# New duration estimates for DMA issues and for per-partition operands in a kernel that orders its own instructions

## The chip, the cores and the metric

The kernel runs on one core of a Trainium2 chip. The metric is the time of one execution on the device in microseconds (us), as the median of several runs. A profile is one execution seen by the hardware profiler. TensorE appears in it as PE (matmuls) and PEld (weight loads), VectorE as DVE, ScalarE as ACT, GpSimd as POOL, and SyncE, which issues all DMAs of this kernel, as SP.

## The reference

The reference is a bucketed attention followed by a mixture of four attention experts, for 4 batches, 8 heads, 768 positions, head size 64:

```
# attention: q, k, v are (4, 8, 768, 64); proj is (64, 6)
mask = bucket(q @ proj > 0)[..., :, None] == bucket(k @ proj > 0)[..., None, :]
scores = where(mask, q @ k.T / 8, -1e9)
x = softmax(scores) @ v            # heads side by side: (4, 768, 512)
# mixture: 4 experts, causal attention, the best 2 of 4 count
logits = x @ w_gate
for e in range(4):
    a = softmax(where(causal, -1e9, (x @ wq[e]) @ (x @ wk[e]).T / 8))
    ye = a @ (x @ wv[e]) @ wo[e]
    out += (weight of e among the two best gates, else 0) * ye
```

## The kernel before

**Units.** The work is cut into units: 32 L units (one head of one batch of the first attention) and 16 M units (one expert of one batch). For each unit TensorE computes the scores twice: once to find the row maxima (tile mx, reduced by VectorE into pm), once transposed (tile st) for the exponentials (p and ph by ScalarE, their difference pl by GpSimd), and then the product with V (tile o), which VectorE divides (xp, yn). Numbers are kept as a half-precision part and a remainder, so a product takes three matmuls.

**Preparation of a pair of heads.** For a pair, natq, natk and natv are loaded from DRAM (`load`; the load of natv may not come before the preparation of another pair has made its tile M, which `nc.gate` ensures). `pair_scales` reduces natq, natk and natv to their largest magnitudes (mqk) on VectorE and passes these through TensorE (tile misc) to a scale cs. `prep_pair` transposes and scales q and k; VectorE's scalar_tensor_tensor reads the scale as a per-partition operand. `signs` makes M, with two such operands, and sends four pieces of it by DMA into the qk tiles. `halves` sends eight copies from qk to qk. `shift_steps` sends the maxima (row) and flags (fr) by DMA. An M unit (`proj_steps`) has five transfers of its own, the constant rows01 and four copies. Results leave through ot, p32 or Tq.

**The order of the instructions.** Nothing of this is run as it is written down. Every call is recorded as an operation with its predecessors; then `schedule` lists the operations for the five engines. It keeps a time at which each engine comes free, takes the operation that can start earliest on it (ties by program order with some offsets), and adds the operation's estimated cost, which is `_cost`. The order in which operations were taken is the order in which each engine runs them. So an estimate never changes an instruction's real duration; it changes what is listed before what. Some copies have two engines to choose from (`copy`, `choose`), and that choice also goes by the estimated times.

A DMA's estimate has two parts. The issue takes SP's time, which is the part that is edited. The transfer then lands after

```
            free[e] = end = st + cost
            if o.dma is not None:
                dma = end = max(dma, st + 1275.0) + o.dma
                end += 900.0
```

counted from st, the start of its issue. For a load of natv (384 KB in pieces of 256 bytes) `o.dma` is 2,185 ns by the formula in `add`, and a reader on another engine adds 60 and 75 ns, which makes 4.50 us from issue to use. On the chip each engine runs its list strictly in order: if an operation's input is late, everything listed behind it on that engine waits as well.

In the profile every instruction carries the line at which the listed operations are issued (L423), so that groups are told apart by tiles: `qk<-M` reads M and writes qk.

Of the kernel before, what the change touches and what calls it, by code (L numbers as in the profile page):

```python
# [156 lines left out]
def _n(v):  # L157
    return prod(v.shape[1:])


def _cost(rec, eng, name, out, ins, args, kw):
    if name == "dma_start":
        return 650.0
    n = max([_n(out)] + [_n(x) for x in ins[:1]]) if eng != "tensor" else _n(out)
    psum = any(x.tile.space for x in ins if isinstance(x, View))
    if eng == "tensor":
        w = ins[0].dtype
        if name == "transpose":
            return 112.0
        if w == FT:  # L170
            return max(216.0, n * 1.68) / (4 if kw.get("tile_position") else 1)
        if w == FR:
            return max(107.0, n / 2.4 + 3)
        return max(28.0, n / 2.4 + 3) / (4 if kw.get("tile_position") else 1)
    ptr = sum(1 for x in list(args[2:]) + list(kw.values())
              if isinstance(x, View) and x.dtype == FT and prod(x.shape) == x.shape[0])
    if name == "reg_load":
        return 250.0
    if eng == "scalar":
        return (51.0 if psum else 93.0) + 0.833 * n + 93 * ptr  # L180
    if eng == "vector":
        if name == "memset" or (not psum and len([x for x in ins if _n(x) > 1 or n == 1]) < 2
                                and name != "tensor_reduce" and out.dtype != HF):
            return 66.0 + n / 1.92 + 60 * ptr
        return 64.0 + n / 0.96 + 20 * ptr
    if eng == "gpsimd":
        if name == "tensor_tensor":
            return (135.0 if n == 128 else 80.0 + (-0.36 * n if out.tile.name in ("xp", "yn") else 0.0)) + (2.0 if out.dtype == HF else 2.2) * n
        if name == "memset":
            return 36.0 + 0.83 * n if out.dtype in (FT, FR) and n > 200 else 40.0 + 0.1 * n  # L190
        return 190.0 + 2.0 * n
    raise ValueError(eng)
# [12 lines left out]
class Recorder:  # L205
# [21 lines left out]
    def add(self, alts):  # L227
# [9 lines left out]
        o.prio = o.i  # L237
        o.tag = self.tag
        o.alts = [(e, m, a, k, _cost(self, e, m, o.outs[0] if o.outs else None, o.ins, a, k)) for e, m, a, k in alts]
        o.dma = None  # L240
        o.bias = POOL_BIAS
# [1240 lines left out]
```

## Time and profile before

| | |
|---|---|
| time, median of 3 runs | 654.75 us (652.87 to 656.1) |
| the profiled execution's own time | 658.51 us |
| its span, first to last instruction | 656.5 us |
| mean granted TensorE clock | 0.994 of full speed |
| PE busy | 625.3 us, 95% of the span |
| DVE, ACT, POOL busy | 78%, 77%, 70% |
| DMA queue's packets | 32.1% of the 16 engines' time |

Sums of waits and durations below come from the profiled execution, and are then set against the median. A wait in the profile is idle time of an engine just before an instruction, with the event that ended it.

### The profile page before, as it was taken

How to read it: one execution, taken by the hardware profiler on the slowest of the kernel's cores; microseconds unless marked ns; L12 is line 12 of the kernel's file. 1: busy time of each engine (PE TensorE's matmuls, PEld its weight loads, DVE VectorE, ACT ScalarE, POOL GpSimd, SP SyncE). 2: the span in 40 equal slices, each digit the busy share in tenths (PEclk: the TensorE clock that was granted, in tenths of full speed). 3: DMA queues.
4: the chain of work that ended last, by engine and by line, in shares of the span. 5: the costliest groups of instructions: out<-in, count | busy, mean ns of one | idle time of the engine just before them, and what ended most of it. 6: DMA issues, size and time to landing. Idle time of an engine off the chain costs nothing.

```text
span 656.5 us, 21599 instructions
## 1 busy us (share of the span) xinstructions
PE 625.3 (95%) x8297; PEld 459.5 (70%) x8297; DVE 512.1 (78%) x1303; ACT 503.6 (77%) x1106; POOL 462.0 (70%) x509
## 2 busy tenths in 40 slices
PE   8989999898999999999999989899999999999996
PEld 7877767665767676776667767677776766767663
DVE  4997999998779797968879777886977968437653
ACT  3299988998969798867868869685985977952774
POOL 4099988997959686956957769774893867970550
PEclk9999999999999999999999989989999999999999
DMA  4682554443411505032342333305044121001212
GB/s 104 146 176 66 108 118 102 99 100 88 107 41 29 120 19 132 19 84 65 67 116 75 69 78 67 87 15 132 12 89 126 44 70 26 4 19 34 79 66 97
DMA packets 110883, 50.88 MB, mean 77 GB/s; under 512 B 89388, under 2 KB 106940, under 8 KB 110780
## 3 DMA queue, kind: packets, MB, share of 16 engines
q1 hardware_dynamic: 110780, 49.50, 32.1%
q8 instruction: 65, 1.06, 0.7%
q14 instruction: 38, 0.31, 0.2%
HBM read 20.98 MB, written 6.29 MB: 42 GB/s over the span
## 4 chain that ended last, share of the span: by engine, by line
PE 63%; DVE 15%; DMA 10%; ACT 4%; issue 3%; SPq 3%; POOL 1%; DVEq 0%; POOLq 0%; ACTq 0%
PE misc L423 21%; PE st L423 16%; PE o L423 16%; PE mx L423 10%; DVE pm L423 6%; DMA natv<-in_v_dram 5%; SPq L423 3%; DMA qk<-M 2%; ACT p L423 2%; DVE qk L423 2%; DVE mqk L423 2%; ACT ph L423 1%; DVE misc L423 1%; DMA natk<-in_k_dram 1%; POOL pl L423 1%
## 5 line engine op out<-in xcount | busy, mean ns | idle before, releaser
L423 POOL TENSOR_TENSOR pl<-p,ph 128x512 f16<-128x512 f32 x379 | 418.9, 1128 | 169.5 <-ACT ph L423 77.1
L423 ACT ACTIVATE p<-st 128x512 f32<-128x512 f32 (+2 forms) x384 | 227.0, 593 | 53.3 <-PE st L423 45.2
L423 DVE TENSOR_REDUCE pm<-mx 128x2 f32<-128x512 f32 (+2 forms) x380 | 226.9, 615 | 16.9 <-PE mx L423 15.6
L423 PE MATMUL st<-qk 78*128 78x512 f16 (+2 forms) x976 | 228.0, 324 | 1.9 <-ACT ph L423 0.8
L423 ACT ACTIVATE ph<-st 128x512 f16<-128x512 f32 (+2 forms) x384 | 227.0, 596 | 0.5 <-PE o L423 0.4
L423 PEld LDWEIGHTS <-ph 128*128 128x128 f16 x2976 | 157.8, 98 | 27.7 <-issue 3.8
L423 PEld LDWEIGHTS <-qk 78*128 78x128 f16 (+4 forms) x1392 | 124.0, 98 | 62.2 <-issue 10.4
L423 PE MATMUL mx<-qk 76*128 76x512 f16 (+2 forms) x488 | 136.1, 325 | 5.9 <-DVE pm L423 3.1
L423 PEld LDWEIGHTS <-pl 128*128 128x128 f16 x1488 | 136.2, 97 | 5.0 <-issue 1.5
L423 PE MATMUL o<-vh,ph 128*128 128x65 f16 (+1 forms) x1152 | 125.7, 194 | 0.6 <-DVE xp L423 0.4
L423 PE MATMUL o<-vh,pl 128*128 128x65 f16 (+1 forms) x1152 | 125.5, 193 | 0.6 <-POOL pl L423 0.6
L423 PE MATMUL o<-vl,ph 128*128 128x64 f16 x1152 | 125.3, 192 | 0.1
L423 PE MATMUL misc<-xt,wqk_h 128*128 128x384 f16 x256 | 53.7, 326 | 1.3 <-DVE ytl L423 1.3
L423 PEld LDWEIGHTS <-ident 128*128 128x128 bf16 x460 | 36.2, 102 | 13.1 <-issue 2.8
L423 DVE SCALAR_TENSOR_TENSOR qk<-misc,qk 128x384 f16<-128x384 f32 (+1 forms) x34 | 18.7, 552 | 27.0 <-ACT qk L423 26.9
L423 PE MATMUL o<-mvh,ph 128*128 128x65 f16 x336 | 37.7, 195 | 0.6 <-DVE yn L423 0.6
L423 PEld LDWEIGHTS <-xt 128*128 128x128 f16 x324 | 30.3, 97 | 11.3 <-issue 1.0
L423 PE MATMUL o<-mvh,pl 128*128 128x65 f16 x336 | 37.6, 195 | 0.0
L423 PE MATMUL o<-mvl,ph 128*128 128x64 f16 x336 | 37.6, 193 | 0.0
L423 ACT ACTIVATE qk<-misc 128x384 f16<-128x384 f32 (+1 forms) x33 | 16.2, 490 | 27.2 <-PE misc L423 24.1
L423 PEld LDWEIGHTS <-wqk_h 128*128 128x128 f16 x256 | 24.2, 97 | 15.4 <-issue 1.0
L423 DVE SCALAR_TENSOR_TENSOR qk<-misc,cs,qk 128x384 f16<-128x384 f32 x56 | 33.2, 604 | 1.3 <-ACT qk L423 1.2
(188 smaller groups left out, 930.1 us busy)
## 6 DMA issues: line engine op xcount, KB each, us to landing
qk<-qk SPq DMA_DIRECT2D x128, 96.0 KB
natv<-in_v_dram SPq DMA_DIRECT2D x16, 384.0 KB
natq<-in_q_dram SPq DMA_DIRECT2D x15, 384.0 KB
natk<-in_k_dram SPq DMA_DIRECT2D x15, 384.0 KB
qk<-qk SPq DMA_DIRECT2D x112, 48.0 KB
out_dram<-ot SPq DMA_DIRECT2D x20, 256.0 KB
xt<-xt SPq DMA_DIRECT2D x8, 96.0 KB
xt<-xt SPq DMA_DIRECT2D x4, 192.0 KB
```

The lines of the kernel that those rows point to most:

```text
L423: getattr(getattr(self.nc, e), m)(*[real(x) for x in args], **{k: real(x) for k, x in kw.items()})
```

## The change

No operation is added or removed. Two estimates in `_cost` are edited: the SP time of a DMA's issue, one constant before, now depends on the tile that is read; and each per-partition fp32 operand of a VectorE instruction that falls under the last line of that branch adds 60 ns where it added 20. Loads from DRAM have no tile that is read, and fall under 570.

```
     if name == "dma_start":
-        return 650.0
+        of = ins[0].tile.name if ins else ""
+        return 930.0 if of in ("M", "Mw") else 700.0 if of[:3] in ("row", "fr") else 340.0 if of in ("ot", "p32") else 570.0
...
-        return 64.0 + n / 0.96 + 20 * ptr
+        return 64.0 + n / 0.96 + 60 * ptr
```

## Rows read from the trace of the kernel before

**Rows 1.** The page: busy time of each engine, and share of the span.
```profile
PE 625.3 (95%) x8297; PEld 459.5 (70%) x8297; DVE 512.1 (78%) x1303; ACT 503.6 (77%) x1106; POOL 462.0 (70%) x509
```

**Rows 2.** Waits of PE: total us, times, longest us.
```profile
PE misc L423 <- DVE mqk L423: 4.5, 3, 2.8
PE misc L423 <- DVE row L423: 3.4, 3, 1.5
PE mx L423 <- DVE pm L423: 3.1, 10, 0.7
PE mx L423 <- DMA qk<-M: 1.6, 3, 1.1
```

**Rows 3.** Waits of DVE: total us, times, longest us.
```profile
DVE mqk L423 <- DMA natv<-in_v_dram: 15.9, 10, 3.2
DVE mqk L423 <- DMA natq<-in_q_dram: 6.1, 6, 2.2
```

**Rows 4.** Chain of work that ended last, near one natv: start us, us, what.
```profile
382.56 0.60 SPq L423
...
383.20 4.09 DMA natv<-in_v_dram
...
387.32 0.97 DVE mqk L423
...
388.33 0.23 PE misc L423
```

**Rows 5.** Windows around ten natv waits: length, PE, PEld, DVE, ACT, POOL busy, PEclk, DMA.
```profile
384.00:390.00 6.00, 3.17 (x49) 2.18 (x46) 2.81 (x7) 2.40 (x7) 3.89 (x4) 0.97 0.42 94
...
sum 62.00, PE 49.41 PEld 34.06 DVE 42.08 ACT 38.06 POOL 39.65; mean PE 4.94 PEld 3.41 DVE 4.21 ACT 3.81 POOL 3.97
```

**Rows 6.** SP's issues before that natv: start us, us, tiles, count.
```profile
368.69 5.98 SPq L423 DMA_DIRECT2D qk<-M  x4
374.71 2.45 SPq L423 DMA_DIRECT2D qk<-qk  x4
377.27 0.71 SPq L423 DMA_DIRECT2D qk<-row  x1
378.10 5.06 SPq L423 DMA_DIRECT2D qk<-qk  x7
383.20 0.59 SPq L423 DMA_DIRECT2D natv<-in_v_dram  x1
```

**Rows 7.** SP's issues before the natv at 116 us.
```profile
111.08 3.66 SPq L423 DMA_DIRECT2D qk<-M  x4
114.78 0.66 SPq L423 DMA_DIRECT2D qk<-row  x1
115.49 0.64 SPq L423 DMA_DIRECT2D fq<-fr  x1
116.17 0.40 SPq L423 DMA_DIRECT2D natv<-in_v_dram  x1
```

**Rows 8.** SP's issues before the natv at 177 us.
```profile
169.73 3.66 SPq L423 DMA_DIRECT2D qk<-M  x4
173.45 3.50 SPq L423 DMA_DIRECT2D qk<-qk  x4
176.99 0.59 SPq L423 DMA_DIRECT2D natv<-in_v_dram  x1
```

**Rows 9.** SP's issues before the natv at 297 us.
```profile
285.59 4.42 SPq L423 DMA_DIRECT2D qk<-M  x4
290.06 0.66 SPq L423 DMA_DIRECT2D qk<-row  x1
290.76 5.03 SPq L423 DMA_DIRECT2D qk<-qk  x8
295.84 0.79 SPq L423 DMA_DIRECT2D qk<-rows  x1
296.68 0.42 SPq L423 DMA_DIRECT2D natv<-in_v_dram  x1
```

**Rows 10.** DVE groups by shape: out<-in, count | busy us, mean ns | idle before.
```profile
L423 DVE SCALAR_TENSOR_TENSOR qk<-misc,cs,qk 128x384 f16<-128x384 f32 x56 | 33.2, 604 | 1.3 <-ACT qk L423 1.2
...
L423 DVE SCALAR_TENSOR_TENSOR qk<-misc,qk 128x384 f16<-128x384 f32 x32 | 17.7, 552 | 26.9 <-ACT qk L423 26.9
```

**Rows 11.** Issues of stores from ot: ns min/median/max, first and last start.
```profile
L423 SPq DMA_DIRECT2D out_dram<-ot x20: 332/338/537, 334.8 to 651.9; - x20
```

**Rows 12.** Windows behind two natv waits: PE busy, ..., PEclk (granted clock).
```profile
388.00:394.00 6.00, 5.61 (x62) 3.89 (x63) 5.24 (x16) 3.12 (x8) 2.55 (x3) 0.72 0.02 3
426.00:432.00 6.00, 5.34 (x58) 3.84 (x58) 5.04 (x16) 4.07 (x10) 2.67 (x3) 0.72 0.02 5
```

## The prediction

> **What bounds the kernel now.** I read the page's busy times first. TensorE is busy 625.3 of 656.5 us [rows 1]: 31.2 us are all that a better order could win, since the work stays. Next, PE's waits say where those 31 us lie. The largest are matmuls into misc that wait for VectorE (mqk, row), then mx behind pm, then mx behind the transfer of M [rows 2]. So the next question is what VectorE itself waits for. The one DMA that stops it often is natv, 15.9 us in ten waits; natq adds 6.1 us [rows 3].
>
> The chain of work shows how such a wait reaches TensorE: SP issues natv, it lands 4.09 us later, VectorE reduces it for 0.97 us, and only then PE's next misc matmul starts [rows 4]. VectorE had been idle, because mqk stood at the head of its list and everything behind it had to wait. Windows of 6 us (one of 8) around the ten waits tell the price: PE is busy 49.41 of 62 us, so 12.6 us of its idle time lie there, against 15.9 us of VectorE's waits, 0.79 us for each us [rows 3, 5]. This is an upper bound, as some of that idle has other causes.
>
> Why is natv late? Not for its landing: the list allows 4.50 us from issue to use, and the transfer took 4.09 [rows 4]. It is issued late. In front of it on SP stands an unbroken run of issues that begins with four of M. At 369 us it is 16 issues long and took 14.5 us [rows 6], where 16 times 650 ns is 10.4: 4.1 us late. The other forms: 4 of M, row and fr, 5.1 us against 3.9 [rows 7]; 4 of M and 4 copies, 7.3 against 5.2 [rows 8]; 14 issues, 11.1 against 9.1 [rows 9]. An issue of M takes 0.92 us, start to start [rows 7], a copy 0.635 (8 in 5.08) and rows01 0.84 [rows 9]. So M is what the old constant had far wrong; for a copy 650 was good.
>
> **The change part by part.** No instruction is added, so the price of each edit is what it does to waits.
>
> *Issues before natv.* The list now counts 930 for M (+280), 700 for row, fr and rows01 (+50), 570 for a copy (-80). The planned start of natv moves later by 1.22 us in the run of [rows 7] (1.12 + 0.10), 0.80 in [rows 8] (1.12 - 0.32), 0.58 in [rows 9] (1.12 + 0.10 - 0.64) and 0.29 in [rows 6] (1.12 + 0.05 - 0.88). I counted the runs before all ten waits: one is worth 1.22, three 0.80, four 0.58 and two 0.29. Together that is 1.22 + 2.40 + 2.32 + 0.58 = 6.5 us. If VectorE's list gets useful work for all of that, PE gains 6.5 x 0.79 = 5.1 us. If nothing was ready to be listed earlier, it gains 0. I take half, 2.6: PE is still busy 80% of those windows [rows 5], so work exists, but not for every one.
>
> *M's landing.* PE waits 1.6 us in three places for M [rows 2]. Its last piece is now planned 0.84 us later (3 x 280), which covers two of the three waits and most of the longest, 1.1. Ends 0 and 1.6; I take 1.2, because other matmuls stand ready in nearly every stretch.
>
> *VectorE's operands.* With a per-partition operand the instruction on 384 columns takes 604 ns, without it 552 [rows 10]: 52 ns, nearer 60 than 20. By the groups of the same view about 240 such operands run, 56 of them in the form shown, so the list gives VectorE 240 x 40 ns = 9.6 us more, spread over the span. Chains of two to four of them come before a pm or a misc, 0.1 to 0.2 us; the ten waits for pm are 0.3 us on average [rows 2]. Ends 0 and 2; I take a gain of 0.5. Some copies may also move from VectorE to ScalarE; both have over a fifth of their time free [rows 1], so I cost that at nothing.
>
> *What gets worse.* Loads of natq and natk are now planned at 570 with the rest, 80 ns closer together, and natq already waits six times [rows 3]. Six times 50 to 80 ns is up to 0.5 us; I take a loss of 0.3. Stores fall from 650 to 340, against 338 measured [rows 11]: truer, and nothing waits for them; nothing. Copies fall to 570 against 635. Their cover is that they are listed early enough: no row of PE's waits names qk<-qk. That is why I cost them at nothing; without the cover they are the second rival.
>
> The Trainium skill, page "DMA: Bandwidth & Descriptors", section "Issuing engines are not separate DMA queues", says that the time a sequencer needs to start a DMA is usually small beside the DMA itself. Were that so here, the issue estimates would hardly matter and the sum would keep only the operands' 0.5 us. The trace disagrees: 14.5 us of issues stand before a transfer of 4.09 us [rows 4, 6].
>
> The sum: -2.6 - 1.2 - 0.5 + 0.3 = -4.0 us. The profiled execution took 658.51 us, its span 656.5; by it the changed kernel takes 654.5. That execution was 3.8 us above the median of the runs, so I apply the difference to the median: 654.75 - 4.0 = 650.75 us, 650.8 rounded.
>
> **The rivals.** *Nothing comes of it.* A list order is a chain of near ties, and a shift of 80 ns early in the program regroups all that follows. New small waits may appear where old ones went, so that gains and losses cancel; or the orders stay much alike, and the edit does little. For it: the longest wait, 3.2 us [rows 3], is hardly touched by its 0.29 us. Against it: the mean shift, 0.65 us, is two fifths of the mean wait, 1.6. Time: 654.5.
>
> *SP runs behind its list.* This one ends on the other side. The list now lets SP issue a copy in 570 ns where it takes 635 [rows 9]. After the eight copies of a pair it is 0.52 us ahead of the chip; 14 pairs make 7.3 us. If the matmuls that read these copies are listed right after their planned landing, each pair costs up to 0.5 us of PE. It decides from the point where the slack between a copy's landing and its first reader falls under 0.5 us. For it: the old 650 was above 635 and left no such lag. Against it: PE never waits for qk<-qk today. At the full price, with half of the gains above, the time is 654.75 + 7.3 - 2.0 = 660.1; at half the price and no gain 658.4. I put 658.5. A long wait would cost more than itself: behind two natv waits, with PE standing for 2.8 us in the first [rows 2], the granted clock was 0.72 for 6 us [rows 12], that is partly at 1.2 instead of 2.4 GHz, 1.7 us lost in each. The same rows give the low end: if both of those waits go, 3.4 us come back.
>
> **How the numbers follow.** A measurement of this kernel tells about 0.5% (3.3 us) from no change. The forecast, faster by more than that: 0.47. Nothing comes of it, within 0.5%: 0.31. SP behind, or another new wait, slower by more: 0.22. Low end of the range: all bounds together, 5.1 + 1.6 + 2.0 + 3.4 = 12.1 us, 642.7. High end: 660.1. These hold the three cases but for the rare reshuffle beyond both. The forecast's own range is 642.7 to 651.4.
>
> **What would show it.** Right: DVE's waits for natv fall from 15.9 us to about 10, PE's waits for M to under 0.6, PE's idle time in the span from 31 to 27 us, with busy times of all engines unchanged within 1%. On SP the runs before natv stay as long as they are; what changes is which VectorE work precedes mqk. The operand edit shows as fewer than ten short waits of mx for pm. Wrong: waits of PE for qk<-qk, rows01 or row appear (the second rival), or natv's waits fall and PE's idle time does not, because it moved to other releasers (the first). The prediction fails above all if a long wait appears or goes with its stretch of low clock, which alone is worth 3 to 5 us.

## The result and the profile after

The changed kernel took 659.73 us (median of 8 executions, 656.07 to 665.21) beside 654.32 us of the kernel before: a ratio of 1.008, 95% interval 1.0051 to 1.0108. Measured again later it took 659.47 us beside 654.82, ratio 1.0058 (1.0025 to 1.009). It is slower by 0.6 to 0.8%, where 0.6% faster was forecast. Ratios, and the averages further down, but not the medians, leave out executions more than 1.5% above the fastest of their kernel: seven of 29 of the kernel before on chip 1 below, which lowers its average there by 1.0 us, two of 35 on chip 2 and none elsewhere.

The profiled execution after took 659.3 us, its span 657.5. Every engine's order is new, though no operation is. The page's busy times, to be set beside [rows 1]:

```profile
PE 627.6 (95%) x8307; PEld 461.2 (70%) x8307; DVE 509.0 (77%) x1297; ACT 504.3 (77%) x1112; POOL 461.4 (70%) x509
```

PE's idle time went down, from 31.2 to 29.9 us. Its busy time went up by 2.3 us for the same matmuls; ten more of them, small filler, are too little for that (the list itself puts short throw-away matmuls into gaps that it foresees). When the same work takes longer, the clock is the first suspect. Before that, the waits of PE that answer to [rows 2] (total us, times, longest):

```profile
PE misc L424 <- DVE mqk L424: 5.0, 3, 2.6
PE mx L424 <- DVE pm L424: 3.3, 10, 0.5
PE st L424 <- ACT ph L424: 3.0, 7, 0.9
PE st L424 <- DMA qk<-row: 2.9, 3, 1.8
...
PE mx L424 <- DMA qk<-M: 0.7, 1, 0.7
```

And those of VectorE that answer to [rows 3]:

```profile
DVE mqk L424 <- DMA natv<-in_v_dram: 9.2, 5, 2.9
...
DVE mqk L424 <- DMA natq<-in_q_dram: 4.3, 5, 1.7
```

The waits aimed at did shrink: natv from 15.9 to 9.2 us, M from 1.6 to 0.7. But two others have grown in PE's list: for ph from 0.8 to 3.0 us, and for row from 0.8 to 2.9. Before, they read:

```profile
PE st L423 <- ACT ph L423: 0.8, 2, 0.5
PE st L423 <- DMA qk<-row: 0.8, 1, 0.8
```

SP's run before the natv at 385 us shows the estimates at work (start, us, tiles, count; compare [rows 6]):

```profile
371.89 4.37 SPq L424 DMA_DIRECT2D qk<-M  x4
376.31 0.54 SPq L424 DMA_DIRECT2D qk<-qk  x1
376.90 0.67 SPq L424 DMA_DIRECT2D qk<-row  x1
377.61 7.40 SPq L424 DMA_DIRECT2D qk<-qk  x10
385.06 0.59 SPq L424 DMA_DIRECT2D natv<-in_v_dram  x1
```

The list now plans these 16 issues at 10.7 us; they took 13.2. It is 2.5 us short where it was 4.1. Of that, the plan grew by 0.3 us only; the rest is that these issues took 1.3 us less than in [rows 6]. VectorE's operand is unchanged work (compare [rows 10]):

```profile
L424 DVE SCALAR_TENSOR_TENSOR qk<-misc,cs,qk 128x384 f16<-128x384 f32 x56 | 32.8, 604 | 0.8 <-ACT qk L424 0.7
```

Now the clock. These are windows around three stretches; behind the length come the busy us of PE, PEld, DVE, ACT and POOL, then PE's granted clock, the DMA share and its GB/s:

```profile
116.00:120.00 4.00, 2.65 (x13) 1.14 (x13) 3.27 (x6) 4.00 (x9) 3.76 (x5) 0.88 0.71 164
120.00:126.00 6.00, 6.00 (x52) 3.88 (x51) 3.80 (x7) 4.24 (x12) 5.52 (x5) 0.51 0.61 133
388.00:391.00 3.00, 0.84 (x9) 0.42 (x6) 1.54 (x3) 1.11 (x4) 2.52 (x3) 1.00 0.17 39
391.00:397.00 6.00, 5.57 (x65) 4.08 (x65) 5.33 (x18) 4.02 (x9) 1.81 (x2) 0.72 0.00 0
425.00:428.00 3.00, 0.40 (x6) 0.21 (x3) 1.11 (x3) 1.43 (x4) 2.09 (x3) 1.00 0.45 105
428.00:434.00 6.00, 4.91 (x45) 3.36 (x45) 5.17 (x16) 2.11 (x5) 0.67 (x1) 0.72 0.02 4
```

The last two pairs are the known pattern of [rows 12]: PE stands behind a late natv, and then the granted clock averages 0.72 for 6 us. The first pair is of another kind. PE did not stand there for longer than 0.8 us at once (for ph); it ran thin, busy 2.65 of 4 us, and its clock was 0.51, so at 1.2 GHz, for nearly all of the next 6 us. A second profile of the changed kernel has the same fall there (0.50). The kernel before had almost the same thin stretch at the same time in its profiled execution, and kept its clock:

```profile
116.00:120.00 4.00, 2.79 (x27) 1.69 (x27) 3.33 (x6) 4.00 (x11) 3.36 (x4) 1.00 0.60 138
120.00:126.00 6.00, 5.76 (x69) 3.56 (x66) 5.83 (x20) 5.99 (x16) 6.00 (x6) 1.00 0.52 119
```

It does not always keep it. In the profile of a later run with the same list (the kernel before with PE kept busy at 388 and 425 us only), the clock falls here too, for less long:

```profile
116.00:120.00 4.00, 3.15 (x27) 1.75 (x27) 3.27 (x6) 4.00 (x11) 3.72 (x4) 0.91 0.63 148
120.00:126.00 6.00, 6.00 (x66) 4.30 (x65) 5.29 (x19) 4.83 (x13) 6.00 (x6) 0.77 0.49 111
```

So the stretch at 116 us does not belong to the new order alone.

Each execution's result has its span and its mean granted clock. The span times (1 - clock) is the time lost at the lower clock, and the time less that loss I call the time at full clock. The split is an estimate: the mean clock also covers the last microseconds, when PE has no matmul left, and in the profiles 0 to 1.2 us of the loss lie there and cost nothing. Within one kernel on one chip, over all 219 executions, the time rises by 0.86 us for each us of this loss. Over its first eight executions the changed kernel's clock ran from 0.979 (665.21 us, the slowest) to 0.992 (656.07 us, the fastest).

By this split the profiled execution of the kernel before was an unusual one: 658.51 us at a clock of 0.994 is 654.6 us at full clock, where that kernel averages 650 to 651 (table below). Its 31.2 us of PE idle time and 15.9 us of natv waits come from it. The later profile with the same list has 23.8 us (with 52 matmuls more) and 11.5, and a second profile of the changed kernel has 31.3 and 11.4. So the fall of PE's idle time from 31.2 to 29.9 us, and the size of the fall in natv's waits, are not shown to be the change's doing.

### The profile page after: what moved, and what is told of

Its sections match the earlier page's. It is cut to its first block, busy times and chain, and to the rows that moved or that the text cites. A ratio compares the mean times of both kernels' runs of the same rounds, so it can differ in the third digit from the quotient of the medians.

```text
span 657.5 us, 21612 instructions
## 1 busy us (share of the span) xinstructions
PE 627.6 (95%) x8307; PEld 461.2 (70%) x8307; DVE 509.0 (77%) x1297; ACT 504.3 (77%) x1112; POOL 461.4 (70%) x509
## 4 chain that ended last, share of the span: by engine, by line
PE 74%; ACT 9%; DVE 8%; DMA 4%; issue 3%; POOL 1%; SPq 1%; ACTq 0%; POOLq 0%; DVEq 0%
PE misc L424 25%; PE st L424 20%; PE o L424 18%; PE mx L424 11%; ACT p L424 3%; ACT ph L424 3%; DVE pm L424 3%; DMA natv<-in_v_dram 2%; DMA qk<-row 1%; DVE mqk L424 1%; DMA xt<-xt 1%; DVE misc L424 1%; SPq L424 1%; POOL pl L424 1%; DVE rden L424 1%
## 5 line engine op out<-in xcount | busy, mean ns | idle before, releaser
L424 PEld LDWEIGHTS <-ph 128*128 128x128 f16 x2976 | 159.9, 98 | 27.6 <-issue 2.1
L424 PE MATMUL mx<-qk 76*128 76x512 f16 (+2 forms) x488 | 137.7, 327 | 5.6 <-DVE pm L424 3.3
L424 PE MATMUL o<-vh,pl 128*128 128x65 f16 (+1 forms) x1152 | 126.9, 194 | 1.4 <-POOL pl L424 1.3
L424 ACT ACTIVATE qk<-misc 128x384 f16<-128x384 f32 (+1 forms) x30 | 14.7, 490 | 28.2 <-PE misc L424 26.2
```

The source lines that it names most:

```text
L424: getattr(getattr(self.nc, e), m)(*[real(x) for x in args], **{k: real(x) for k, x in kw.items()})
```

## The experiments

Three theories were put to the test. **A**: the new order makes TensorE stand or run thin where the clock then falls, and the loss is mostly time at the lower clock. **B**: SP runs behind its list because copies are now planned too short, which was the prediction's second rival. **C**: any reshuffle scatters the time by some microseconds, and what the estimates say plays no part. A run's chip stands in brackets; the first run's chip is not known, and its own reference (654.32 us) has no clock on record.

All results in one table; the ratio is to the kernel before on the same chip, the last three columns are averages over the executions.

| kernel | median us | ratio (95%) | clock | lost at lower clock, us | at full clock, us |
|---|---|---|---|---|---|
| before, chips 1 / 2 / 3 | 655.36 / 657.58 / 654.82 | | 0.993 / 0.991 / 0.992 | 4.8 / 6.0 / 5.4 | 650.0 / 651.3 / 650.1 |
| changed, first | 659.73 | 1.008 (1.0051, 1.0108) | 0.987 | 8.7 | 651.2 |
| changed, again (chip 3) | 659.47 | 1.0058 (1.0025, 1.009) | 0.988 | 8.1 | 651.6 |
| issue estimates alone (1) | 654.96 | 1.0003 (0.9975, 1.0032) | 0.994 | 4.1 | 650.5 |
| operand estimate alone (1) | 660.93 | 1.0115 (1.0067, 1.0163) | 0.991 | 6.2 | 655.0 |
| distances as measured (1) | 650.61 | 0.9935 (0.9904, 0.9966) | 0.999 | 1.0 | 649.8 |
| the same again (3) | 650.17 | 0.9927 (0.9893, 0.9961) | 0.999 | 0.5 | 649.9 |
| the same, 5 ns less for copies and loads (2) | 658.05 | 1.0014 (0.9985, 1.0044) | 0.992 | 5.2 | 653.2 |
| changed, copies and loads at 640 (2) | 655.49 | 0.9968 (0.9936, 0.9999) | 0.995 | 3.3 | 651.9 |
| natv planned later (2) | 655.16 | 0.9964 (0.9933, 0.9996) | 0.995 | 3.2 | 651.9 |
| changed, PE busy in two places (1) | 656.32 | 1.003 (0.9998, 1.0062) | 0.993 | 4.5 | 651.3 |
| changed, PE busy in three places (2) | 654.36 | 0.9946 (0.9916, 0.9976) | 0.996 | 2.5 | 651.7 |
| before, PE busy in two places (3) | 653.22 | 0.9968 (0.9937, 0.9999) | 0.996 | 2.5 | 650.5 |

**Each half of the change alone.** First only the issue estimates:

```
-        return 64.0 + n / 0.96 + 60 * ptr
+        return 64.0 + n / 0.96 + 20 * ptr
```

> The issue estimates of the change alone; the operand estimate stays at 20 ns. Theory A (the new order lets TensorE stand still or run thin in stretches that bring the granted clock down to half, and the added low-clock time is the loss; the waits for natv did fall as foreseen): if the issue estimates make that order, waits for natv near 9 us, a third stretch of low clock, 658 to 661 us. Theory B (SP runs behind its list because copies are estimated at 570 ns and take 635): 658 to 661 us as well, but with PE waiting for qk<-qk. Theory C (any reshuffle of a list of near ties scatters by some microseconds, and the estimates' meaning plays no part): anywhere from 650 to 662 us.

Then only the operand estimate, in the kernel before:

```
-        return 64.0 + n / 0.96 + 20 * ptr
+        return 64.0 + n / 0.96 + 60 * ptr
```

> The operand estimate of the change alone; every issue stays at 650 ns. Theory A: no new stretch of low clock where the M issues are not moved; 652 to 656 us, natv waits still near 16 us. Theory B: SP's list is as before, so 653 to 656 us. Theory C: anywhere from 650 to 662 us.

The issue estimates alone give no measurable difference. The natv waits fall to 9.1 us as in the whole change, and nothing is gained. Theory A's and B's 658 to 661 us were a miss. The operand estimate alone costs 1.15%, which A and B had at no loss, and most of that stands at full clock. A expected its natv waits near 16 us; they were 9.9, although every issue was still planned at 650. So a fall of this size needs no new estimate for M. These waits of PE grew most (compare [rows 2]; row had 0.8 us):

```profile
PE mx L423 <- DVE pm L423: 7.8, 16, 1.8
PE st L423 <- DMA qk<-row: 7.3, 5, 2.5
```

The halves do not add up either: alone one loses nothing and the other 4 to 5 us at full clock, together they lose about 1 us at full clock and the rest at the lower clock. An edit's part in the loss can't be told by undoing it.

**The distances as the trace has them.** The estimates of the change are the durations of issues for copies, stores and rows, but the start-to-start distance for M. Here all are distances:

```
-        return 930.0 if of in ("M", "Mw") else 700.0 if of[:3] in ("row", "fr") else 340.0 if of in ("ot", "p32") else 570.0
+        return 930.0 if of in ("M", "Mw") else 850.0 if of == "rows01" else 770.0 if of[:3] in ("row", "fr") else 440.0 if of in ("ot", "p32") else 640.0
```

> The whole change, with the issue estimates set to the start-to-start distances of the trace: 930 for M, 850 for rows01, 770 for row and fr, 440 for stores, 640 for copies and loads; operands at 60 ns. Theory B: SP is no longer ahead of the chip in its list, so the loss goes: 650 to 654 us. Theory A: the time follows the low-clock stretches that the order happens to have, whatever the copies cost; with as many as in the changed kernel 657 to 661 us. Theory C: anywhere from 650 to 662 us.

650.61 us is 0.65% below the kernel before and 9 us below the changed kernel. Taken alone that speaks for B. But only 1.4 us of the 9 stand at full clock (651.2 against 649.8). The rest is the clock: this order hardly ever brings it down. Two controls followed. One moves the estimate by 5 ns, which means nothing to SP:

```
-  ... else 640.0
+  ... else 635.0
```

> The estimates at the start-to-start distances, with copies and loads at 635 ns instead of 640, a difference without meaning that still regroups the list. If the truth of the estimates is what made 650.6 us, this comes within 2 us of it, 648.5 to 652.5. Theory C: it falls anywhere from 650 to 662 us, more likely above 653 than not.

It came out at 658.05 us on a chip where the kernel before took 657.58, so nothing of the gain is left (1.0014 against 0.9935), with waits of 6.6 us for pm and a clock of 0.992. That is theory C's case: the gain did not come from truer estimates as such. The other control undoes in the change what B blames, and with it the same estimate for loads:

```
-  ... else 570.0
+  ... else 640.0
```

> The changed kernel with the estimate of copies and loads at 640 ns instead of 570, everything else of the change kept. Theory B (the copies estimated too short make SP run behind its list, and that is the loss): the loss of 5 us goes, 649 to 654 us. Theory A (the loss is the time at the lower clock that an order happens to bring): the time minus the time lost at the lower clock stays within 2 us of the changed kernel's 651.2, and the time itself follows the clock. Theory C (scatter of reshuffles): anywhere from 650 to 662 us.

655.49 us misses B's 649 to 654, and its time at full clock, 651.9 us, is that of the changed kernel within 0.7. What it gained on the changed kernel it gained in clock (3.3 us lost, not 8). PE waits nowhere for qk<-qk in the changed kernel's profile. Its waits for row did grow, which the prediction had also named as a sign of this rival; but they are no smaller with copies at 640:

```profile
PE st L424 <- DMA qk<-row: 4.3, 4, 1.5
```

With the issue estimates alone, which keep copies at 570, nothing was lost. So copies planned too short are not the loss by themselves. Whether they helped to make the order whose clock falls, these runs can't tell.

The fast order was then measured again, since its neighbour was so far off:

> The fastest version so far once more on another day and chip, since its nearest neighbour came out 7 us slower: if its order seldom brings the clock down, its mean granted clock is again above 0.997 and the time 5 to 8 us below the changed kernel's on the same chip; if the first measurement was a lucky one, it lies within 2 us of the kernel before.

It held: 650.17 us, clock 0.999, 9.3 us below the changed kernel on the same chip, of which 7.6 us are clock. In both its profiles the clock stays at 1.00 until PE's last matmul. An order is a lottery ticket, but the same ticket pays again.

**Is a wait for natv worth what the prediction charged?** In the kernel before, the list counts a reader of natv as 1.5 us later; nothing else is touched:

```
+        o.late = 1500.0 if eng0 == "sync" and o.outs and o.outs[0].tile.name == "natv" else 0.0
...
-                        r = max(r, p.end + (LAT["dma"] + WAIT if p.dma is not None else
+                        r = max(r, p.end + (LAT["dma"] + WAIT + p.late if p.dma is not None else
```

> The kernel before with one thing added to the list's arithmetic: a reader of natv is counted 1,500 ns later than the transfer is estimated to land; issue and operand estimates as before. The prediction's step (each us of VectorE's waits for natv costs TensorE up to 0.79 us): the waits for natv fall from 15.9 to under 5 us, TensorE's idle time falls by 4 us or more, 647 to 652 us. Theory C: the waits fall, and the time falls anywhere from 650 to 662 us.

VectorE's waits for natv all but went, as the first line shows, and then PE's list of waits:

```profile
DVE mqk L424 <- DMA natv<-in_v_dram: 3.0, 3, 1.6
```

```profile
PE st L424 <- DMA qk<-row: 6.3, 7, 1.7
PE mx L424 <- DVE pm L424: 4.1, 9, 0.7
...
PE mx L424 <- DMA qk<-M: 1.8, 2, 1.2
```

At full clock nothing was gained: 651.9 us against 651.3 of the kernel before on that chip. With 13 us less of waiting for natv, PE's waits for row are 6.3 us, which had been 0.8, and those for pm 4.1 (3.1). One order is one draw of the lottery, but the others say the same. Orders with 15.9, 9.1, 3.6 and 2.5 us of natv waits (before, issue estimates alone, distances, 5 ns less) took 650 to 651, 650.5, 649.8 and 653.2 us at full clock: no link. The waits of mx for pm go with that time better: 3.1 us for before and distances, 6.6 and 7.8 for the two orders slowest at full clock (653.2 and 655.0). That is a link over single profiles, not a shown cause. What the kernel did gain, 0.4%, lies in the clock (3.2 us lost against 6.0).

**Is it the clock?** If so, more work in the right places must save time. In the changed kernel 32 matmuls of 128 columns were put into PE's finished order just before each of the two matmuls that stand for mqk at 390 and 428 us; what they write is overwritten.

```
+            if o in self.extra:
+                order += [(o, self.extra[o][1])] * self.extra[o][0]
             order.append((o, a))
...
+                nc.extra[o] = (warm, ("tensor", "matmul", (p[:, 0:128], ident16, ident16), dict(start=True, stop=True), 55.0))
```

> The changed kernel with the same order, and 32 more matmuls of 128 columns, about 1.8 us of TensorE work, just before the matmul that waits for mqk at about 390 us and at about 428 us (64 in all; their results are overwritten). Theory A: TensorE no longer stands still there for 2.0 and 2.6 us, the clock stays at full speed behind both places, and the time falls by up to 1.7 us for each, to 656 to 658 us, although work was added. Theories B and C: the added work fills waits or lengthens them; 659.5 to 662 us, not less.

The windows, in the same columns as above:

```profile
116.00:120.00 4.00, 2.92 (x19) 1.66 (x19) 3.24 (x7) 4.00 (x10) 3.78 (x4) 0.85 0.71 163
120.00:126.00 6.00, 6.00 (x56) 3.84 (x54) 4.04 (x12) 3.95 (x10) 5.17 (x6) 0.53 0.59 132
387.00:390.00 3.00, 2.86 (x46) 2.45 (x43) 1.55 (x3) 1.42 (x5) 2.83 (x3) 1.00 0.24 50
390.00:396.00 6.00, 5.53 (x75) 3.61 (x75) 6.00 (x21) 4.85 (x11) 2.24 (x3) 1.00 0.00 0
424.00:427.00 3.00, 1.90 (x27) 1.35 (x25) 3.00 (x9) 0.10 (x1) 0.74 (x1) 1.00 0.02 3
427.00:433.00 6.00, 6.00 (x92) 4.57 (x89) 5.90 (x18) 5.78 (x13) 3.65 (x4) 1.00 0.02 4
```

Behind both places the clock is at 1.00 where it was 0.72; the thin stretch at 116 us, left alone, still halves it. 64 matmuls were added and the median fell by 3.4 us, to 656.32 (the ratio from 1.008 to 1.003; the intervals overlap a little). The time at full clock is the changed kernel's, 651.3. Then 44 small matmuls, which add zeros to an accumulator, were put into the thin stretch as well:

```
+                order += [(last, ("tensor", "matmul", (last.outs[0], self.thin[o][1], self.thin[o][2].to_broadcast([128, w])),
+                                  dict(start=False, stop=False, skip_group_check=True), 28.0))] * self.thin[o][0]
...
+THIN_ST = {(6, 7): 4, (7, 0): 24}
+THIN_MX = {(8, 1): 8, (8, 2): 8}
```

> The changed kernel with the two groups of 32 extra matmuls, and 44 more of 64 columns that add zeros to an accumulator, put where TensorE runs thin between 116 and 119 us (about 1.2 us of work). Theory A: the stretch of low clock that begins at 119 us and lasts 6.8 us goes as well, which is worth 2 to 3 us on average: 652 to 654.5 us, with a mean granted clock above 0.995. Theories B and C: 656 to 658 us, the added work costs or does nothing.

```profile
116.00:120.00 4.00, 3.58 (x62) 2.34 (x59) 3.25 (x6) 4.00 (x10) 3.74 (x5) 1.00 0.61 142
120.00:126.00 6.00, 5.91 (x81) 4.21 (x81) 6.00 (x19) 6.00 (x17) 6.00 (x7) 1.00 0.53 118
```

The halved clock behind the thin stretch is gone, the loss averages 2.5 us, and with all that added work the changed kernel's order beats the kernel before, by 0.54%. The mean clock over the executions is 0.996, above the 0.995 expected. In this one profile the clock fell all the same in two other stretches, at 94 us and behind the second filled place (0.75 from 424 to 427 us, PE busy 1.95 of 3 us): the filling works on the average and not in every execution. A is the main cause of the loss against the kernel before; no run put the same matmuls where PE was already busy. Last, the same filling in the kernel before, 32 and 20 matmuls at its own two places:

> The kernel before with the same order, and 32 and 20 extra matmuls of 128 columns just before the matmuls that wait for mqk at about 388 and 425 us (results overwritten), where its profile shows 2.8 and 1.5 us of standing and a halved clock behind. Theory A: work is added and the time falls, by up to 1.7 us for each place, 2 to 4 us below the kernel before on the same chip. Theory C: nothing but added work, the same time or up to 3 us more.

It gained 0.3% (0.9968), 2.1 us by the ratio, at the low end of what A expected: the loss halved from 5.4 to 2.5 us. Its window at the first place reads `1.00` where [rows 12] have 0.72:

```profile
390.00:396.00 6.00, 6.00 (x78) 4.63 (x77) 5.67 (x20) 5.96 (x14) 4.57 (x5) 1.00 0.06 13
```

At the second place, with 20 matmuls, the clock was not kept:

```profile
422.00:428.00 6.00, 5.66 (x65) 4.16 (x66) 5.15 (x18) 3.98 (x10) 2.73 (x3) 0.72 0.00 1
```

And the changed kernel once more, beside the kernel before on the same chip, for the account:

> The changed kernel as it is, beside the kernel before and two others on one chip. Theory A: its time minus the time lost at the lower clock is 651 to 652 us, as that of the kernel before on the same chip within 1 us, and the loss at the lower clock is 2 us or more above that of the kernel before. Theory B or C: the two kernels lose the same at the lower clock, and the difference of 5 us stands in the time at full clock.

On that chip the averages are 655.5 and 659.6 us, 4.1 apart: 2.7 us of it lost at the lower clock (5.4 and 8.1), 1.4 at full clock (650.1 and 651.6, with standard errors of 0.3 and 0.5). So two thirds of the loss are the clock. The full-clock part is a little more than A allowed, 1 us, and hardly more than the split can tell.

## Why the prediction was wrong

Beside the kernel before on chip 3, the changed one came out 4.1 us slower where 4.0 us faster was forecast: 8.1 us apart. Of these, 5.4 us are gain at full clock that did not come (4.0 forecast, 1.4 lost), and 2.7 us are clock.

**Natv, the largest gain.** The rows were read rightly: four M stand before natv on SP and hold it up. Its waits fell to 9.2 us where about 10 was foretold, but that number is in part luck: the second profile of the same order has 11.4, and the operand estimate alone, with M at 650, has 9.9. The M of [rows 6] also took 1.5 us each, and 1.1 in [rows 9], so 930 was the low end. The step that failed is the exchange rate, "PE gains 6.5 x 0.79 = 5.1 us", of which half was taken, 2.6 us. The natv waits were thought to be PE's idle time at a discount. Planning natv later took 13 us of these waits away and gained nothing at full clock (651.9 us against 651.3), and over all orders that time does not go with natv's waits. So the idle time in the windows of [rows 5] was not to be had by shortening them. That another late input, row or pm, then stops PE is what its list of waits suggests; no run shows it place by place.

**M's landing.** PE's waits for M fell from 1.6 to 0.7 us: 0.9 of the 1.2 foretold, and not under 0.6, the sign that was named. It is weak support, since the order of the kernel before has 1.1 us in its other profile and the operand estimate alone 0.2. No gain at full clock is seen.

**The operands.** Wrong. The estimate is nearer to the chip (52 ns measured), yet waits of mx for pm stayed at ten, and alone the edit costs 1.15%. A truer price for one kind of instruction gave a worse order here. Where a gain of 0.5 us was taken, the run with this edit alone is 5.0 us slower at full clock.

**What gets worse.** Loads and stores did nothing that can be seen, as costed: natq's and natk's waits together were 7.4 us and are 6.5. Where the prediction says of the issues that the trace disagrees, it sets sixteen of them beside one transfer. One issue alone, natv's, took 0.59 us beside its transfer's 4.09 [rows 4, 6], which is small; what counted was sixteen in a row.

**The low clock.** This is the term that the sum did not have. It stood in the prediction only as the price of a long wait, 1.7 us for each, in the low end of the range, and as the thing that would make the forecast fail. It should have been a term: the kernel before loses 5 to 6 us to it on average, more than the forecast gain, and the changed order adds 3 us to that, more than any single gain that was costed. And the clock fell where PE's longest wait was 0.8 us, so counting long waits would not have found the stretch at 119 us.

The Trainium skill, page "TensorE: Matmul & The Clock Gate", section "Part 1: The HAM clock gate", has the clock halved by default and released by activity. The trace agrees where PE stood (0.84 of 3 us busy, then 0.72), and shows the same fall after PE was busy 2.65 of 4 us.

**The rivals.** SP behind its list, which was given the slower time, is not shown: PE never waited for qk<-qk, with copies at 640 the time at full clock is the same, and the issue estimates alone, with 570, lost nothing. Its number, 658.5, came near the measured one by luck. "A chain of near ties" came closest: a list moved by 5 ns in one estimate gave a ratio of 0.9935 or 1.0014. That should have had more of the chance, on both sides. What stays open is why one order loses its clock more often than another, which the thin stretch at 116 us, common to several, does not tell, and where the last 1.4 us at full clock go; the new waits for ph and row in the profile after are of that size, but no run took them away.

## What to carry to other kernels

Where a planner decides the order, a better estimate is a reshuffle first and an improvement second: judge it by several neighbouring values, measured, before believing the one that won. Split each measured time into the time lost at the lower clock and the time at full clock, with the span and granted clock of each execution, before explaining a change of under 1%. Where TensorE is the bound and runs thin for a few microseconds, filling the stretch with throw-away matmuls can pay on average; here 108 of them took the changed kernel from a ratio of 1.008 to 0.9946.

## What was not expected of the hardware

The same program's time follows its granted clock from run to run: executions of the kernel before ran from 648.48 us at clock 1.000 to over 658 us at 0.988, of the changed kernel from 656.07 at 0.992 to 665.21 at 0.979. Which thin stretch costs the clock is not the same in each execution: with the list of the kernel before, PE was busy 2.79 of 4 us at 116 us in one profile and kept the clock, and busy 3.15 of 4 in another and lost it.
